# Channel mixing of a Fourier layer: three products per chunk against four products per pair of chunks

## The chip, the cores and the metric

The kernel runs as one program on one core of a Trainium2 chip. The metric is the device time of one execution in microseconds. TensorE (PE in the profile, PEld for its weight loads), VectorE (DVE), ScalarE (ACT), GpSimd (POOL) and SyncE (SP, which issues most transfers) each run their own instruction list in order and wait for each other through semaphores.

## The reference

Three layers follow one another. The change lies in the first, which works on eight batches of 3072 positions and 256 channels:

```python
X = np.fft.rfft(x, axis=1)                 # x: 8 x 3072 x 256
Yr = Xr @ w_r - Xi @ w_i + b_r             # w: 256 x 256
Yi = Xr @ w_i + Xi @ w_r + b_i
Yr = sign(Yr) * max(abs(Yr) - 0.01, 0)     # the same for Yi
y  = np.fft.irfft(Yr + 1j*Yi, n=3072, axis=1)
```

The second layer (`moe`) mixes all 24576 rows of y softly into 32 slots (softmax of `y @ phi` over the positions, and over the slots), sends the slots through eight small expert networks and spreads them back. The third (`moe2`) is a gated network with 1536 hidden units over all rows: RMS norm, `silu(g) * val`, `w_out`. The weights of `moe2` arrive as 64-bit floats.

## The kernel before

**Two stages.** `phase1` does everything up to the slots, without ever forming y: it computes the logits and the slot inputs from the spectrum. Short expert work follows (a class `Mid`, and the first part of `phase2`), and then `phase2` runs the gated network in 48 identical rounds. The change lies in `phase1` alone, apart from a buffer number in the middle part.

**What a batch goes through in `phase1`.** The transform is done in two steps. Step A (`emit_A`) multiplies 16 half tiles of x by a 96x96 table, as three products of split numbers: a value v is written as hi + lo, both in a rounded 32-bit format that TensorE takes fast (fp32r), and hi*hi, hi*lo, lo*hi are summed. `split_hi` rounds on ScalarE (line 218), `split_lo` subtracts on GpSimd (line 223). The result goes to DRAM and comes back turned (`load_B`). Step B (`emit_B`) multiplies it by the second table in full fp32, for six chunks q of 512 spectrum columns, each in two halves h of 128 channels. The mixing (`emit_M`) applies w_r and w_i, adds the bias and applies the threshold. `emit_T` turns the result for the slots, and `emit_L` makes the logits' spectrum with phi. A chain of some 30 small steps (`chain`) then turns logits into softmax weights and adds the batch to the running slot sums; it runs one batch behind, between the mixing of the next batch.

**The mixing in three products.** For each chunk, `emit_B` puts both the spectrum and the sum of its real and imaginary part through the split: line 281 writes lo, line 288 the sum `sm`, lines 291 and 294 the sum's hi and lo. Each of the 36 unit steps of a batch does six products of 256 columns (line 302): w_r on the sum into `psR`, and two difference matrices (`wh_d`, `wh_n`) into the two halves of `psI`, which has one buffer. ScalarE copies `psR` with the bias (lines 324, 325), VectorE adds `psI` (line 337), clips to +-0.01 (line 340), and GpSimd subtracts the clipped part (line 344), which is the threshold.

**What sets the order.** The code writes out each engine's order by hand. A loop of 288 unit steps u (36 per batch) issues a sixth of a chunk's mixing per step; `post` delays evacuations by one or more steps; the list at the end of `chain` puts each chain step at a step number. The chain's knot is: `dmax` (VectorE, line 429), `dpar` (GpSimd's maximum over partitions, line 433), `dmn` and `dsub` (VectorE, lines 442 to 452, which need it), `dexp` (ScalarE, line 457), `fa` (TensorE, line 509). The conversion of the 64-bit weights (`converter`, lines 132 to 153) is cut into 121 pieces. A running estimate of VectorE's load decides in which steps a piece is issued.

```python
return [(8, clear), ..., (16, L(dmax, 0, 32)), (17, L(dpar, 32)), (18, L(dmn, 32)),
        (18, L(dsub, 0, 32)), (19, L(dexp, 0, 32)), (19, alexp), (20, L(fa, 0, 16), 1), ...
```

Of the kernel before, what the change touches and what calls it, by code (L numbers as in the profile page):

```python
# [157 lines left out]
def phase1(tc, x, w_r, w_i, b_r, b_i, phi, t_d, t_bf, t_ci, t_ai, t_af, t_id,  # L158
# [46 lines left out]
    def split_hi(g, dve=False):  # L205
        b, i, h = g // 16, g // 2 % 8, g % 2
        if b == 0 and i % 2:

            if h == 0:
                xsp["t"] = xq_p.tile([128, 2, 2, 512], F32R, name="xq")[0:96]  # L210
            xs = xsp["t"][:, h, 0, :], xsp["t"][:, h, 1, :]
# [46 lines left out]
    def emit_B(b, q, h):  # L258

        t = bin_t[b, q]  # L260
        o = 2 if q else 0
        if h == 0:
            xq[b, q] = xq_p.tile([128, 2, 2, 512], F32R, name="xq")
            sq[b, q] = xq_p.tile([128, 2, 2, 258], F32R, name="sq")
        X, S = xq[b, q], sq[b, q]
# [5 lines left out]
        w4 = lambda a: a.rearrange("p (r j k) -> p r j k", j=4, k=32)  # L271
        hi, lo = [w4(X[:, k, h, :]) for k in range(2)]
        xi = xi_p.tile([128, 256], F32, name="xi")
        sm = xi_p.tile([128, 258], F32, name="sm")
# [22 lines left out]
        for k, f in enumerate((evac, rest, s_hi, s_lo)):  # L297
            post(f, 1 + k, int(k < 2))

    def products(ps, key, ch, V, w0, w1):  # L300
        for n, (w, k, h) in enumerate(((wh, 0, 0), (wh, 0, 1), (wl, 0, 0), (wl, 0, 1), (wh, 1, 0), (wh, 1, 1))):
            nc.tensor.matmul(out=ps, lhsT=w[key][:, h, 128 * ch:128 * ch + 128], rhs=V[:, k, h, w0:w1],  # L302
                             start=(n == 0), stop=(n == 5))

    def emit_M(b, q, m):

        X, S = xq[b, q], sq[b, q]
        ch, g = divmod(m, 3)
        if m == 0 and q % 2 == 0:
            if (b, q) == (NB - 1, 4):  # L310

                yy[b, 2] = mid.early.rearrange("p (a h f) -> p a h f", a=2, h=2), 0
            else:
                yy[b, q // 2] = y_p.tile([128, 2, 2, 514], F32, name="yy"), 2
        Y, y0 = yy[b, q // 2]
        o = 2 if q else 0
        Y = Y[:, q % 2, ch, o + y0 - 2:]
        if g == 0:
            ps = psR.tile([128, 512], F32, name="psR")
            products(ps[:, o:258], "r", ch, S, o, 258)  # L320
            v = mix["v"] = v_p.tile([128, 514], F32, name="v")

            def first():
                nc.scalar.activation(out=v[:, o:258], in_=ps[:, o:258], func=AF.Identity, bias=bias[:, 0, ch:ch + 1])
                nc.scalar.activation(out=v[:, 258:514], in_=ps[:, 2:258], func=AF.Identity, bias=bias[:, 1, ch:ch + 1])
            post(first)
            return
        if g == 1:
            mix["ps"] = psI.tile([128, 512], F32, name="psI")
            products(mix["ps"][:, 256:512], "d", ch, X, 0, 256)  # L330
            return
        ps, v = mix["ps"], mix["v"]
# [871 lines left out]
```

## Time and profile before

| what | value |
|---|---|
| three runs | 1872.07, 1874.18, 1877.80 us (median 1874.18) |
| the profiled execution | 1873.3 us, of which 1871.5 us are the span of the trace |
| busy in the span | PE 1744.1, weight loads 1548.1, DVE 1441.1, ACT 1154.0, POOL 408.2 us |
| start, up to the loop's first mixing product | 0 to 41.1 us |
| the loop of `phase1`, eight batches | 41.1 to 702.6 us: 66.4, 90.8, 85.9, 91.3, 89.6, 91.5, 85.7, 60.3 us |
| last chain, experts, start of the third layer | 702.6 to 786.1 us |
| the gated network | 786.1 to 1871.5 us, PE busy 1080.6 of 1085.4 us |

The boundaries of the batches are the start times of the first mixing product of each. The first batch has no chain beside it, the last no step A. The gated network has TensorE busy all the time at the full clock. In the loop no engine is busy all the time, and the granted clock of TensorE lies below 1.0.

### The profile page before, as it was taken

The numbers are of one execution on the slowest core, as the hardware profiler recorded it, in microseconds if no ns is written. First come the engines' busy times: TensorE is split into PE (matmuls) and PEld (weight loads), VectorE is DVE, ScalarE is ACT, GpSimd is POOL, SyncE is SP. The second block draws the span as 40 slices with busy tenths as digits, with TensorE's granted clock in tenths as the row PEclk, the third lists the DMA queues.
The fourth block names the chain that finished last, engine by engine and source line by source line (L and its number), as shares of the span: only waits on it lengthen the run. The fifth ranks groups of instructions, "written<-read, shape, count | busy, mean of one in ns | idle before, by whom it ended". The sixth has DMA issues, their size and how long they took to land.

```text
span 1871.5 us, 35164 instructions
## 1 busy us (share of the span) xinstructions
PE 1744.1 (93%) x13422; PEld 1548.1 (83%) x13422; DVE 1441.1 (77%) x2399; ACT 1154.0 (62%) x2451; POOL 408.2 (22%) x338
## 2 busy tenths in 40 slices
PE   7897889788888888999999999999999999999999
PEld 5776767576766764699999999999999999999998
DVE  5997988888897975677777777778777778778775
ACT  4764656464655543776676676666676676676653
POOL 3665555545564431100000000000000000000000
PEclk9998989898989999999999999999999999999999
DMA  9774635354554539702302302302302303202101
GB/s 238 225 190 119 178 111 164 113 164 124 156 161 136 164 104 308 215 24 62 61 24 63 60 23 63 60 24 63 63 25 67 64 23 75 48 24 57 28 19 35
DMA packets 134489, 183.57 MB, mean 98 GB/s; under 512 B 39232, under 2 KB 103248, under 8 KB 134320
## 3 DMA queue, kind: packets, MB, share of 16 engines
q1 hardware_dynamic: 133584, 179.36, 36.2%
q8 instruction: 105, 1.72, 0.4%
q0 software_dynamic: 624, 1.92, 0.4%
q14 instruction: 64, 0.52, 0.1%
q10 hardware_dynamic: 112, 0.04, 0.0%
HBM read 102.62 MB, written 66.06 MB: 90 GB/s over the span
## 4 chain that ended last, share of the span: by engine, by line
PE 58%; DVE 1%; DMA 1%; issue 0%; SPq 0%; ACT 0%; POOL 0%; DVEq 0%
PE pe L1101 21%; PE po L1101 21%; PE pg L1063 7%; PE pv L1065 7%; PE psx L848 1%; DMA wo<-wo_d 1%; DVE hl L97 1%; DMA cs<-ct_d 0%; PE pm L889 0%; PE pm L906 0%; PE psB L558 0%; PE psx L1101 0%; DVE h L1069 0%; SPq L855 0%; PE pm L848 0%
## 5 line engine op out<-in xcount | busy, mean ns | idle before, releaser
L1069 DVE TENSOR_TENSOR h<-s,pv 128x512 f32<-128x512 f32 x576 | 394.2, 685 | 268.4 <-ACT s L1067 267.6
L1067 ACT ACTIVATE s<-pg 128x512 f32<-128x512 f32 x576 | 344.5, 598 | 346.8 <-PE pg L1063 344.5
L1101 PE MATMUL pe<-wo,hh 128*128 128x256 f32 x2304 | 426.9, 279 | 0.3
L1101 PE MATMUL po<-wo,hh 128*128 128x256 f32 x2280 | 421.9, 279 | 0.0
L1101 PEld LDWEIGHTS pe<-wo,hh 128*128 128x128 f32 x2304 | 381.3, 188 | 42.2 <-DVE o L1117 3.0
L97 DVE TENSOR_TENSOR hl<-h,hh 128x512 fp32r<-128x512 f32 x572 | 405.9, 710 | 0.7 <-ACT s L1067 0.6
L96 ACT ACTIVATE hh<-h 128x512 fp32r<-128x512 f32 x576 | 359.4, 624 | 8.7 <-DVE h L1069 7.8
L1101 PEld LDWEIGHTS po<-wo,hh 128*128 128x128 f32 x2280 | 350.1, 188 | 4.4
L1101 PE MATMUL pe<-wo,hl 128*128 128x256 f32 x1152 | 321.0, 279 | 0.0
L1101 PE MATMUL po<-wo,hl 128*128 128x256 f32 x1140 | 317.7, 279 | 0.0
L1063 PE MATMUL pg<-cq,gst 128*128 128x512 f32 x576 | 229.8, 399 | 0.3 <-ACT s L1067 0.2
L1065 PE MATMUL pv<-cq,gst 128*128 128x512 f32 x576 | 228.0, 396 | 0.7 <-DVE h L1069 0.7
L1101 PEld LDWEIGHTS pe<-wo,hl 128*128 128x128 f32 x1152 | 216.1, 188 | 0.0
L1101 PEld LDWEIGHTS po<-wo,hl 128*128 128x128 f32 x1140 | 213.8, 188 | 0.0
L1039 POOL TENSOR_TENSOR c<-c,ss 128x768 f32<-128x768 f32 x7 | 10.9, 1553 | 842.1 <-DVE ss L1038 842.1
L223 POOL TENSOR_TENSOR xlo<-xraw,xhi 96x512 fp32r<-96x512 f32 x106 | 141.7, 1342 | 65.6 <-issue 28.6
L344 POOL TENSOR_TENSOR yy<-v,p 128x512 f32<-128x512 f32 (+1 forms) x92 | 123.4, 1341 | 114.7 <-DVE p L340 89.2
L302 PE MATMUL psI<-xq,wh_d 128*128 128x256 f32 x384 | 98.7, 340 | 51.9 <-DVE v L337 51.6
L302 PEld LDWEIGHTS psI<-xq,wh_d 128*128 128x128 f32 x384 | 64.7, 205 | 77.9 <-DVE v L337 61.1
L1065 PEld LDWEIGHTS pv<-cq,gst 128*128 128x128 f32 x576 | 108.5, 188 | 2.4 <-DVE h L1069 1.8
L245 ACT ACTIVATE asb<-psA 96x512 f32<-96x512 f32 x109 | 63.8, 586 | 73.9 <-PE psA L242 58.7
L1063 PEld LDWEIGHTS pg<-cq,gst 128*128 128x128 f32 x576 | 108.2, 188 | 1.3 <-ACT s L1067 1.1
(310 smaller groups left out, 2845.3 us busy)
## 6 DMA issues: line engine op xcount, KB each, us to landing
bin<-bounce SPq DMA_DIRECT2D x192, 128.0 KB, 4.0
bounce<-asb SPq DMA_DIRECT2D x59, 384.0 KB, 4.4
xraw<-in_x_dram SPq DMA_DIRECT2D x56, 384.0 KB, 3.9
ex<-in_moe_w_dram SPq DMA_DIRECT2D x16, 1024.0 KB, 10.6
out_dram<-o SPq DMA_DIRECT2D x124, 128.0 KB, 2.2
cs<-ct_d SPq DMA_DIRECT2D x32, 384.0 KB, 7.1
out_dram<-o SPq DMA_DIRECT2D x132, 64.0 KB, 1.7
ct_d<-ch SPq DMA_DIRECT2D x16, 384.0 KB, 3.3
```

The lines of the kernel that those rows point to most:

```text
L96: nc.scalar.activation(out=hi, in_=src, func=AF.Copy)
L97: (lo_eng or nc.vector).tensor_tensor(out=lo, in0=src, in1=hi.bitcast(F32), op=ALU.subtract)
L223: eng.tensor_tensor(out=lo, in0=v, in1=hi.bitcast(F32), op=ALU.subtract)
L245: nc.scalar.activation(out=asb[b, i][:, 512 * h:512 * h + 512], in_=ps, func=AF.Copy)
L302: nc.tensor.matmul(out=ps, lhsT=w[key][:, h, 128 * ch:128 * ch + 128], rhs=V[:, k, h, w0:w1], start=(n == 0), stop=(n == 5))
L344: eng.tensor_tensor(out=Y, in0=v[:, o:514], in1=p[:, o:514], op=ALU.subtract)
L848: nc.tensor.matmul(out=ps[:, 256 * k:256 * k + 256], lhsT=v[:, 128 * (n + k):128 * (n + k) + 128], rhs=sst, start=True, stop=True)
L1063: nc.tensor.matmul(out=pg, lhsT=gst[:, 128 * fb:128 * fb + 128], rhs=v, start=True, stop=True)
L1065: nc.tensor.matmul(out=pv, lhsT=gst[:, 1536 + 128 * fb:1536 + 128 * fb + 128], rhs=v, start=True, stop=True)
L1067: nc.scalar.activation(out=s, in_=pg, func=AF.Silu)
L1069: nc.vector.tensor_tensor(out=h, in0=s, in1=pv, op=ALU.mult)
L1101: nc.tensor.matmul(out=ps, lhsT=a[:, ts], rhs=w[:, fb, :], start=(fb == 0 and k == 0), stop=(fb == 11 and k == 2))
```

## The change

- **Mixing.** Four products instead of three, on pairs of chunks: real and imaginary part, each from w_r and from w_i (or its negative `wh_n`), in groups of 12 products of 512 columns. The groups go through two buffers `psM`, which replace `psR` and `psI`. A unit step now issues four products of 512 columns instead of six of 256. The sums `sm`, their split and the tiles for them are gone.
- **Threshold.** ScalarE writes relu(ps + b - 0.01) straight from PSUM (`first`), and VectorE writes min(ps + b + 0.01, that) from PSUM over it (`end`). Clip and GpSimd's subtraction are gone. The columns of frequency 0 and 1536, which the three-product form treated inside the sums, get four tiny fp32 products of their own (`emit_0`).
- **Conversion.** Its last one or two operations go from GpSimd to VectorE. The rule for when to issue a piece has other numbers: 21 pieces a batch in batches 1 to 5 (16 before, 22 in batch 5), 15 in batch 0 (11 before), and the last of the 121 is issued at step 216 (249 before).
- **Chain.** The steps stand at other numbers: `dmax` 12, `dpar` 13, `dmn` and `dsub` 18, `dexp` 19, `fa` 22 and 23. `dsub` now writes its result turned, so that `fa` reads 512 neighbouring elements instead of elements 32 apart.
- **Loop.** Steps A, B, T and L stand at other places within 12 steps instead of 6. One of the sixteen expert tiles (1 MB each) is loaded after the loop instead of near its end.

```diff
@@ converter
-            nc.gpsimd.tensor_tensor(out=w, in0=w, in1=p.bitcast(F32), op=ALU.mult)
+            v.tensor_tensor(out=w, in0=w, in1=p.bitcast(F32), op=ALU.mult)
...
-                nc.gpsimd.tensor_tensor(out=w, in0=w, in1=h, op=ALU.subtract)
+                v.tensor_tensor(out=w, in0=w, in1=h, op=ALU.subtract)
@@ emit_B
         def evac():
             nc.scalar.activation(out=hi, in_=v, func=AF.Copy)
-            nc.scalar.activation(out=w4(xi), in_=v[:, 2:4], func=AF.Copy)
 
         def rest():
             nc.vector.tensor_tensor(out=lo, in0=v, in1=hi.bitcast(F32), op=ALU.subtract)
...
-            nc.vector.tensor_tensor(out=w4(sm[:, 2:258]), in0=v[:, 0:2], in1=w4(xi), op=ALU.add)
-
-        def s_hi():
-            nc.scalar.activation(out=S[:, 0, h, o:258], in_=sm[:, o:258], func=AF.Copy)
-
-        def s_lo():
-            nc.vector.tensor_tensor(out=S[:, 1, h, o:258], in0=sm[:, o:258], in1=S[:, 0, h, o:258].bitcast(F32), op=ALU.subtract)
@@ emit_M
+        ways = (("r", ri), ("i" if ri else "n", 1 - ri))
+        cs = slice(128 * ch, 128 * ch + 128)
+        if m % 3 < 2:
+            h = m % 3
+            terms = [(w[key][:, h, cs], X[:, 0, h, part]) for key, part in ways for w in (wh, wl)]
+        else:
+            terms = [(wh[key][:, h, cs], X[:, 1, h, part]) for h in range(2) for key, part in ways]
+        for n, (w, v) in enumerate(terms):
+            nc.tensor.matmul(out=ps, lhsT=w, rhs=v, start=(m % 3 == 0 and n == 0), stop=(m % 3 == 2 and n == 3))
...
-        def add():
-            nc.vector.tensor_tensor(out=v[:, 2:514], in0=ps, in1=v[:, 2:514], op=ALU.add)
-
-        def clip():
-            nc.vector.tensor_scalar(out=p[:, o:514], in0=v[:, o:514], scalar1=LAM, scalar2=-LAM, op0=ALU.min, op1=ALU.max)
+        def first():
+            nc.scalar.activation(out=Y, in_=ps[:, o:512], func=AF.Relu, bias=b_lo[:, ri, ch:ch + 1])
 
         def end():
-            eng = nc.vector if (b, q) == (NB - 1, 5) else nc.gpsimd
-            eng.tensor_tensor(out=Y, in0=v[:, o:514], in1=p[:, o:514], op=ALU.subtract)
+            nc.vector.scalar_tensor_tensor(out=Y, in0=ps[:, o:512], scalar=b_hi[:, ri, ch:ch + 1], in1=Y, op0=ALU.add, op1=ALU.min)
@@ chain
-            v = S["d"].rearrange("p (n s) -> p n s", s=32)[:, :, s0:s1]
+            v = S["d"].rearrange("p (s n) -> p n s", n=32)[:, :, s0:s1]
...
-                nc.tensor.matmul(out=ps, lhsT=af, rhs=v[:, k:k + 16], start=True, stop=True)
+                nc.tensor.matmul(out=ps, lhsT=af, rhs=S["d"][:, 32 * k:32 * k + 512], start=True, stop=True)
...
-                    (16, L(dmax, 0, 32)), (17, L(dpar, 32)), (18, L(dmn, 32)), (18, L(dsub, 0, 32)), (19, L(dexp, 0, 32)),
+                    (12, L(dmax, 0, 32)), (13, L(dpar, 32)), (14, cmax), (15, csub), (18, L(dmn, 32)), (18, L(dsub, 0, 32)),
@@ loop
-        load = max(0.0, load + fixed[(u + 1) % 6] + chained.get((u + 1) % 36, 0.0) - (1.7 if u < 6 * (T - 17) else 1.82))
+        load = max(0.0, load + fixed[(u + 1) % 12] + chained.get((u + 1) % 36, 0.0) - pace)
```

**The order on GpSimd around the maximum.** The kernel before, in a middle batch (ISA rows belong to the maximum over partitions, `mb<-mx`; `xlo` is `split_lo`, `yy` the end of the threshold, `cvw` the conversion, `ch<-ch,mc` a later chain step):

```order
L223 TENSOR_TENSOR xlo<-xraw,xhi 96x512
L344 TENSOR_TENSOR yy<-v,p 128x512
L433 ISA
L433 ISA mb<-mx 128x32
L223 ISA
L223 TENSOR_TENSOR xlo<-xraw,xhi 96x512
L344 TENSOR_TENSOR yy<-v,p 128x512
L223 TENSOR_TENSOR xlo<-xraw,xhi 96x512 x2
L344 TENSOR_TENSOR yy<-v,p 128x512
L144 TENSOR_TENSOR cvw<-cvw,cva 128x256
```

The changed kernel at the same place:

```order
L226 TENSOR_TENSOR xlo<-xraw,xhi 96x512 x11
L429 ISA
L429 ISA mb<-mx 128x32
L226 ISA
L226 TENSOR_TENSOR xlo<-xraw,xhi 96x512
L465 TENSOR_TENSOR ch<-ch,mc 96x1024
L226 TENSOR_TENSOR xlo<-xraw,xhi 96x512 x3
L479 TENSOR_TENSOR ch<-ch,sc 96x1024
L226 TENSOR_TENSOR xlo<-xraw,xhi 96x512
L489 TENSOR_TENSOR ch<-ch 96x1024
```

The end of the threshold and the conversion have left GpSimd. Beside the maximum and three chain steps only `split_lo` is left on it.

**The order on VectorE around the wait for that maximum.** The kernel before, from `dmax` to `dsub` (`mn<-mb` is the first instruction that needs the maximum, `v` and `p` belong to the mixing, `cva` to the conversion):

```order
L429 TENSOR_REDUCE mx<-ch 96x32
L132 TENSOR_SCALAR cva<-cvraw 128x256
L133 TENSOR_SCALAR cva<-cva 128x256
L134 TENSOR_SCALAR cva<-cva 128x256
L337 TENSOR_TENSOR v<-psI,v 128x512
L340 TENSOR_SCALAR p<-v 128x512
L442 TENSOR_TENSOR mn<-mb,mn 128x32
L444 TENSOR_TENSOR al<-mn 128x32
L452 TENSOR_TENSOR ch<-ch,mn 96x1024
L281 TENSOR_TENSOR xq<-psB,xq 128x512
```

The changed kernel, the last rows up to the same instruction:

```order
L132 TENSOR_SCALAR cva<-cvraw 128x256
L133 TENSOR_SCALAR cva<-cva 128x256
L134 TENSOR_SCALAR cva<-cva 128x256
L323 SCALAR_TENSOR_TENSOR yy<-psM,b_hi,yy 128x512
L376 STREAM_TRANSPOSE lf<-psT 128x256
L136 SCALAR_TENSOR_TENSOR cva<-cvraw,cva 128x256
L138 TENSOR_SCALAR cve<-cvraw 128x256
L139 TENSOR_SCALAR cve<-cve 128x256
L280 TENSOR_TENSOR xq<-psB,xq 128x4x128
L438 TENSOR_TENSOR mn<-mb,mn 128x32
L440 TENSOR_TENSOR al<-mn 128x32
L448 TENSOR_TENSOR ch<-ch,mn 96x32x32
```

In the changed kernel `dmax` (line 425 there) stands 18 instructions ahead of `mn<-mb`, five unit steps after it; in the kernel before it stands six instructions ahead, two unit steps.

## Rows read from the trace of the kernel before

**Rows 1.** Busy time by stretch: batch 0, 4, 7, the part after the loop.
```profile
core 0: us, PE busy (x) PEld busy (x) DVE busy (x) ACT busy (x) POOL busy (x), PEclk, DMA share, GB/s
41.10:107.50 66.40, 58.90 (x442) 50.86 (x442) 59.35 (x100) 47.98 (x110) 41.67 (x38) 1.00 0.83 225
...
375.50:465.10 89.60, 74.80 (x611) 60.12 (x610) 75.75 (x130) 50.80 (x110) 47.95 (x39) 0.90 0.50 140
...
642.30:702.60 60.30, 52.90 (x530) 43.49 (x529) 42.71 (x76) 27.41 (x63) 21.35 (x17) 0.97 0.48 148
702.60:786.10 83.50, 70.88 (x555) 40.94 (x553) 51.57 (x89) 41.73 (x89) 14.50 (x11) 0.98 0.99 292
```

**Rows 2.** The same view of batch 4 by chunk: the third, fourth and fifth.
```profile
400.00:411.30 11.30, 10.68 (x74) 8.86 (x72) 11.02 (x17) 9.04 (x20) 6.05 (x5) 1.00 0.57 145
411.30:434.20 22.90, 17.20 (x117) 11.90 (x115) 14.42 (x25) 9.60 (x22) 6.98 (x7) 0.78 0.22 73
434.20:450.50 16.30, 12.08 (x94) 10.85 (x91) 15.36 (x28) 7.66 (x17) 10.06 (x9) 0.79 0.57 160
```

**Rows 3.** Waits from 100 to 580 us: total us, times, longest.
```profile
PE psI L302 <- DVE v L337: 42.1, 26, 4.2
...
PE psC L509 <- ACT ch L457: 17.3, 5, 5.2
...
DVE mn L442 <- POOL mb L433: 16.7, 4, 6.5
```

**Rows 4.** Timeline of batch 4: start, us, instruction, idle before it and its releaser.
```profile
417.15 0.45 POOL L433 PARTITION_ALL_REDUCE mb<-mx  x1 [6.38 <-PE psI L302]
417.63 0.19 DVE L442 TENSOR_TENSOR mn<-mb,mn 128x32 f32<-128x32 f32 x1 [4.10 <-POOL mb L433]
...
419.22 1.06 ACT L457 ACTIVATE ch<-ch 96x1024 f32<-96x1024 f32 x1 [5.16 <-DVE ch L452]
...
420.33 2.08 PE L509 MATMUL psC<-ch,af 96*128 96x512 f32 x2 [3.70 <-ACT ch L457]
...
424.74 1.25 POOL L223 TENSOR_TENSOR xlo<-xraw,xhi 96x512 fp32r<-96x512 f32 x1 [7.14 <-issue]
```

**Rows 5.** Timeline of batch 4, TensorE at the full clock: transposes, step B, logits, chain.
```profile
410.04 0.60 PE L365 MATMUL psT<-ident,yy 128*128 128x128 f32 x4
...
410.48 1.06 PE L268 MATMUL psB<-bf,bin 128*128 128x128 f32 x8
...
411.29 0.49 PE L302 MATMUL psR<-sq,wh_r 128*128 128x256 f32 x2
...
414.66 1.07 PE L377 MATMUL psT<-yy,ph 128*32 128x256 f32 x16
...
415.66 0.50 PE L302 MATMUL psI<-xq,wh_n 128*128 128x256 f32 x2
...
435.98 0.86 PE L531 MATMUL psC<-bf,ch 128*32 128x128 f32 x24
```

**Rows 6.** Chain that ended last, start of the gated network: start, us, what.
```profile
786.66 0.70 PE pe L1101 x6
...
788.07 0.23 PE pg L1063
```

**Rows 7.** Groups by line up to 760 us: count, busy, mean ns, idle before.
```profile
L337 DVE TENSOR_TENSOR v<-psI,v 128x512 f32<-128x512 f32 x96 | 65.3, 680 | 3.2 <-PE psI L302 2.9 <-PE psB L268 0.2
...
L340 DVE TENSOR_SCALAR p<-v 128x512 f32<-128x512 f32 x80 | 52.5, 656 | 37.4 <-POOL yy L344 29.3 <-DVE v L337 0.5
...
L294 DVE TENSOR_TENSOR sq<-sm,sq 128x256 fp32r<-128x256 f32 x80 | 49.9, 624 | 3.4 <-ACT sq L291 3.4
...
L288 DVE TENSOR_TENSOR sm<-psB,xi 128x256 f32<-128x256 f32 x96 | 39.8, 415 | 0.4
...
L133 DVE TENSOR_SCALAR cva<-cva 128x256 int32<-128x256 int32 x36 | 36.4, 1011 | 1.2
...
L143 DVE SCALAR_TENSOR_TENSOR cvw<-cvr,cve 128x256 f32<-128x256 int32 x36 | 21.3, 591 | 1.2
```

More of the change, by code (lines that the diff above doesn't have):

```diff
@@ L165, in phase1 @@
     dpool = P(st_c, "bounce", 2, DRAM)
-    psA, psB, psR, psI, psT, psC = (P(st_c, n, b, PSUM) for n, b in
-                                    (("psA", 1), ("psB", 2), ("psR", 1), ("psI", 1), ("psT", 1), ("psC", 1)))
+    psA, psB, psM, psT, psC = (P(st_c, n, b, PSUM) for n, b in
+                               (("psA", 1), ("psB", 2), ("psM", 2), ("psT", 1), ("psC", 1)))
     ch_p, yt_p, sm_p = P(st_c, "ch", 5), P(st_c, "yt", 10), P(st_c, "sm", 2)
@@ L209, in split_hi @@
             if h == 0:
[L210 to L211 removed]
+                xsp["t"] = xq_p.tile([128, 2, 2, 2, 512], F32R, name="xq")[0:96]
+            xs = xsp["t"][:, h, 0, 0, :], xsp["t"][:, h, 1, 0, :]
         else:
@@ L260, in emit_B @@
         t = bin_t[b, q]
[L261 to L265, printed above, removed]
+        if h == 0 and q % 2 == 0:
+            xq[b, q // 2] = xq_p.tile([128, 2, 2, 2, 512], F32R, name="xq")
+        if h == 0 and q == 0:
+            x0[b] = x0_p.tile([128, 2, 2], F32, name="x0")
         ps = psB.tile([128, 512], F32, name="psB")
@@ L270, in emit_B @@
         v = ps.rearrange("p (j r k) -> p r j k", r=4, k=32)
[L271 to L274, printed above, removed]
+        hi, lo = [xq[b, q // 2][:, k, h].rearrange("p a f -> p (a f)").rearrange("p (r z j k) -> p r z j k", r=4, z=2, k=32)[:, :, q % 2]
+                  for k in range(2)]
         def evac():
             nc.scalar.activation(out=hi, in_=v, func=AF.Copy)
-            nc.scalar.activation(out=w4(xi), in_=v[:, 2:4], func=AF.Copy)
         def rest():
@@ L295, in emit_B @@
         if h == 1:
             bin_t.pop((b, q))
[L297 to L312, printed above, removed]
-            else:
[L314 to L326, printed above, removed]
-            return
[L328 to L332, printed above, removed]
-        products(ps[:, 0:256], "n", ch, X, 256, 512)
-        p = p_p.tile([128, 514], F32, name="p")
-        def add():
-            nc.vector.tensor_tensor(out=v[:, 2:514], in0=ps, in1=v[:, 2:514], op=ALU.add)
-        def clip():
-            nc.vector.tensor_scalar(out=p[:, o:514], in0=v[:, o:514], scalar1=LAM, scalar2=-LAM, op0=ALU.min, op1=ALU.max)
-        def end():
-            eng = nc.vector if (b, q) == (NB - 1, 5) else nc.gpsimd
-            eng.tensor_tensor(out=Y, in0=v[:, o:514], in1=p[:, o:514], op=ALU.subtract)
-            if q == 0:
-                nc.gpsimd.tensor_copy(out=Y[:, 258:259], in_=Y[:, 0:1])
-            if ch == 1:
-                xq.pop((b, q))
-                sq.pop((b, q))
-        for k, f in enumerate((add, clip, end)):
-            post(f, (1, 1, 2)[k], (0, 0, 1)[k])
@@ new lines, in emit_0, with first, end @@
+    def emit_0(b):
+        X = x0.pop(b)
+        ps = psB.tile([128, 512], F32, name="psB")
+        for ch in range(2):
+            for h in range(2):
+                nc.tensor.matmul(out=ps[:, 2 * ch:2 * ch + 2], lhsT=wf[:, h, 128 * ch:128 * ch + 128], rhs=X[:, h, :],
+                                 start=(h == 0), stop=(h == 1))
+        Y = yy[b, 0]
+        def first():
+            for ch in range(2):
+                nc.scalar.activation(out=Y[:, :, ch, 0], in_=ps[:, 2 * ch:2 * ch + 2], func=AF.Relu, bias=b_lo[:, 0, ch:ch + 1])
+        def end():
+            for ch in range(2):
+                nc.vector.scalar_tensor_tensor(out=Y[:, :, ch, 0], in0=ps[:, 2 * ch:2 * ch + 2], scalar=b_hi[:, 0, ch:ch + 1],
+                                               in1=Y[:, :, ch, 0], op0=ALU.add, op1=ALU.min)
+        post(first, 1)
+        post(end, 2)
@@ L353, in ysl @@
     def ysl(Y, qs, h, ri, par):
-        f = Y[1] + 256 * ri + 128 * par
-        return Y[0][:, qs, h, f:f + 128]
+        return Y[:, ri, h, 256 * par + 128 * qs.start:256 * par + 128 * qs.stop]
     def emit_T(b, q, ri, ps=None):
@@ L569, in busy @@
         def busy(n):
-            ps = bank(psI, "psI")
+            ps = bank(psM, "psM")
             for _ in range(n):
@@ L635, in load_bf @@
         eng.dma_start(out=bf[:, 4 * q:4 * q + 4], in_=t_bf[:, 4 * q:4 * q + 4])
-    banks = [(psA, "psA"), (psI, "psI"), (psB, "psB"), (psT, "psT"), (psB, "psB"), (psR, "psR")]
+    banks = [(psA, "psA"), (psM, "psM"), (psB, "psB"), (psT, "psT"), (psB, "psB"), (psM, "psM")]
     def split_x(g):
@@ L662, in phase1 @@
     load_B(0, 2)
-    for c in range(-5, 0):
+    for c in range(-6, 0):
         clock[0] = c
```

154 lines of the change are left out of this document (91 added, 63 removed).

## The prediction

> **What bounds the kernel now.** I read the busy time by stretch first. The gated network after 786.1 us is untouched and full of TensorE work, so the change can act in the loop (41.1 to 702.6 us) and in the part after it [rows 1]. In batch 4, which stands for the middle ones, 89.6 us pass with VectorE busy 75.75, TensorE 74.80, ScalarE 50.80 and GpSimd 47.95, and the granted clock is 0.90 on the mean, a mix of the levels 2.4 and 1.2 GHz [rows 1]. No engine is full, so waits decide. By chunk, the fourth takes 22.9 us where the third takes 11.3, with the clock at 0.78 [rows 2].
>
> The waits name two places. TensorE waits for VectorE to free `psI`, 42.1 us from 100 to 580 us, that is in 5.4 batches, 7.8 us a batch [rows 3]. And once a batch the chain closes in on itself: GpSimd stands still for 6.38 us before the maximum over partitions and 7.14 us after it, VectorE waits 4.10 us for it, ScalarE behind that 5.16 us, TensorE behind that 3.70 us [rows 4], and after it the clock is low for a while [rows 2]. In all five batches in this stretch TensorE waits at that place, 17.3 us together [rows 3].
>
> **What TensorE needs in a batch.** At the full clock six products of 256 columns take 0.70 us and one of 512 takes 0.23 [rows 6]; four transposes take 0.44 (410.04 to 410.48), eight instructions of step B 0.81, one `emit_L` 1.0, 24 instructions of `fb` 0.86 [rows 5]; two of the four `fa` instructions take 2.08 [rows 4]. A batch before:
> mixing 216 x 0.117 = 25.3; A 48 x 0.23 = 11.0; B 96 x 0.10 = 9.7; T 12 x 0.44 = 5.3; L 3 x 1.0 = 3.0; `fa` 4.2; the rest of the chain, priced by form, `fb` and the equally large `binv` 1.7 each, the slot products 3.0 at the price of L, `ainv` 0.9, so 7.3. Sum 65.8 us. So 23.8 of the 89.6 us are waits and half clock.
>
> **The change part by part.**
>
> *Four products.* 144 x 0.23 = 33.1 us replace 25.3: +7.8 a batch, on TensorE, which no other work hides once it is the bound.
>
> *`fa` from neighbouring elements.* 4.2 us become 4 x 0.23 = 0.9, if 512 columns then cost what they cost elsewhere: -3.3. Ends: 0 (the price stays) and -3.3. I take the low price, since the other products with neighbouring elements all have it. `emit_0` adds eight tiny instructions, between 0.1 and 0.9 us (at most the transposes' 0.11 each), I take 0.6. TensorE's need: 65.8 + 7.8 - 3.3 + 0.6 = 70.9 us.
>
> *VectorE.* Twelve each of lines 288, 294, 337 and 340 go: 12 x (0.415 + 0.624 + 0.680 + 0.656) = 28.5 us [rows 7]. Twelve `end` come, like line 337 a read of PSUM and one of SBUF over 512 elements: 8.2. Conversion: seven products of 0.59 (line 143, same size) that GpSimd did, 4.1, and five more pieces of three instructions at 0.59, 8.9. The turned `dsub` and the small ones, 1.5. So 75.75 - 28.5 + 8.2 + 4.1 + 8.9 + 1.5 = 70.0. From it comes off what VectorE is held by GpSimd: line 133 takes 1.01 us for 256 elements, line 288 0.415 for as many, and 0.6 of that I read as time held. GpSimd's share falls from 0.54 to some 0.35 (48 us less 21 for 12 subtractions and the conversion, over about 77), so a third of 7 x 5 x 0.6 goes: -7. VectorE 63, between 60 and 70: below TensorE's 70.9, but close.
>
> The Trainium skill ("SBUF — State Buffer", section "SBUF: two separate sides") says that VectorE and GpSimd share one port pair as an exclusive lock, and that a VectorE instruction with two inputs from SBUF takes part in it too. That speaks against moving the conversion's products to VectorE; line 143 with its two such inputs takes 0.59 us against line 288's 0.415, a smaller penalty than line 133's, so the trace agrees in kind. By the rule at its worst each of the seven would wait for a whole `xlo` (1.25 us), 9 us a batch instead of 1.
>
> *ScalarE and GpSimd.* ScalarE loses more than it gains and has 39 us free in batch 4. On GpSimd only `split_lo` and the chain are left; each is wanted two A steps later, which is 36/16 x 2 = 4.5 unit steps, about 9 us at 77 us a batch.
>
> *The chain's new places.* `dpar` is issued five unit steps before `dmn` instead of one, some 10 us against 2.5 (89.6 over 36). GpSimd's 6.38 us before the result lie inside that, and the 7.14 us after it inside the 9 us of the `split_lo` on either side. So VectorE's 4.10 us, and behind it ScalarE's and TensorE's, go. The chunk's excess over the third is 11.6 us, of which 4.0 is `fa`'s own price, so 7.6 us a batch. The price if the cover is gone is rival C. The first load of a batch has five unit steps from the last evacuation of A as before, but shorter ones; I count a microsecond for it among the waits that stay.
>
> *`psM` with two buffers.* `end` is issued two unit steps before its buffer is needed again, so VectorE may lag by some 4 us. That takes the 7.8 us at `psI`. What is late next is VectorE during conversion, and step T at the one-buffer `psT`.
>
> *After the loop.* One more tile of 1 MB goes into a stretch whose transfers are busy at 0.99 and run at 292 GB/s [rows 1]: 3.6 us, between 0 (hidden behind the experts' products) and 3.6; I take 3.6. The start: the first mixing product needs two chunks of step B, +1 us.
>
> **The sum.** Of the 23.8 us of waits and half clock 7.6 and 7.8 go; of the 8.4 left I keep 6, since two engines near each other still trip over the conversion's lumps. A batch with chain and conversion: 70.9 + 6 = 77 us.
> Batches 1 to 5: 449.1 become 385. Batch 6, now without conversion: 85.7 become 74. Batch 0, without chain and with few waits to lose: 66.4 + 7.8 - 4 = 70. Batch 7: 60.3 + 7.8 - 3.3 and its stop at the maximum less, 60. The loop: 661.5 become 589, -72.5. With +4.6 outside: 1873.3 - 67.9 = 1805 us, against the profiled execution's own 1873.3. That lies 0.9 below the median of the runs, which changes nothing here.
>
> **Rivals.**
>
> A, *TensorE alone is the bound*: waits of 1 to 2 us a batch. For it: two buffers everywhere on the mixing, and the clock stays high if TensorE never pauses (third chunk: busy 10.68 of 11.3 us, clock 1.00) [rows 2]. Against: `psA` and `psT` keep one buffer. 5 x 72 + 71 + 67 + 58 = 556 for the loop: 1773 us.
>
> B, *VectorE becomes the bound while it converts*: 70 us of work in order with waits at today's ratio (75.75 of 89.6) is 83 to 84 us a batch. For it: three conversion instructions in a row, over 1 us each when GpSimd is active, and the pieces are now denser. Against: that ratio contains the two waits that go. 5 x 84 + 76 + 72 + 61 = 629: 1845 us.
>
> C, *slower: GpSimd's stop hits TensorE directly*. GpSimd is away for 6.38 + 7.14 us around each maximum, and that stays. If it gets to it late, the `split_lo` behind it come late, TensorE stands at step A, and the half clock follows as in the fourth chunk. 13.5 us exposed, some 5 us for the low clock after it, the 6 that stay: 70.9 + 24.5 = 95 us a batch. It decides the sign from 18.7 us of waits a batch. 5 x 95 + 90 + 74 + 66 = 705: +48, 1921 us. Against: only `split_lo` depends on GpSimd now, and it is two steps ahead. The Trainium skill ("GPSIMD Engine Reference", section "2.1 Instruction dispatch") says that the first call of freshly loaded GpSimd code pays about 6 us with nothing in the profile; the trace agrees, with 6.38 and 7.14 us and no instruction in them, and the change removes neither.
>
> D, *nothing moves*: what the waits give back, the fourth product takes (+7.8), and the order stumbles elsewhere by as much: within 0.3%.
>
> **Chances.** Forecast 0.55, A 0.16, B 0.21, C 0.05, D 0.03. The forecast's own range is 1785 to 1825; the range for all takes in most of A and B: 1768 to 1850. A measurement of this kernel tells about 0.3% from no change. Faster 0.92, same 0.03, slower 0.05.
>
> **What would show it.** Right: batches of 75 to 80 us from one first mixing product to the next; TensorE busy over 0.93 of them at a clock of 0.97 or more; `fa` at a quarter of its time; no wait of VectorE for `mb`; GpSimd's two idle stretches still there, each of 6 to 7 us, with no TensorE wait for `xlo` behind them. Wrong: batches over 82 us with TensorE waiting for `end` or for lo of step B (B), waits for `xlo` over 5 us a batch (C), or a product of 512 columns at more than 0.24 us.

## The result and the profile after

The changed kernel takes 1804.03 us, the median of four runs (1802.13 to 1805.98), against 1875.99 us before (1872.07 to 1882.23): ratio 0.9614, 95% interval 0.9583 to 0.9644. The forecast was 1805. The profiled execution took 1805.45 us, 1803.7 of them in the trace.

Busy time by stretch, the changed kernel: batches 0, 3, 4 and 7, the part after the loop, the gated network (columns as in [rows 1]).

```profile
44.40:112.10 67.70, 66.26 (x378) 52.66 (x377) 39.88 (x78) 40.82 (x76) 27.20 (x26) 1.00 0.84 240
...
266.30:344.20 77.90, 76.02 (x545) 57.10 (x544) 64.51 (x111) 43.10 (x78) 28.25 (x20) 1.00 0.60 171
344.20:421.30 77.10, 75.82 (x545) 57.10 (x544) 63.53 (x103) 43.98 (x82) 27.81 (x20) 1.00 0.62 176
...
569.70:629.90 60.20, 58.33 (x465) 43.44 (x464) 28.68 (x43) 19.69 (x33) 6.69 (x4) 1.00 0.41 127
629.90:718.00 88.10, 73.49 (x565) 45.26 (x564) 51.22 (x87) 43.09 (x94) 14.51 (x11) 0.91 0.99 290
718.00:1803.70 1085.70, 1080.93 (x8134) 1026.82 (x8133) 802.71 (x1298) 714.02 (x1492) 26.62 (x14) 1.00 0.20 45
```

The batches last 67.7, 76.4, 77.8, 77.9, 77.1, 77.0, 71.4 and 60.2 us: the loop went from 661.5 to 585.5 us, -76.0. Around it the start grew by 3.3 us and the part after the loop by 4.6; the gated network stayed (1085.4 and 1085.7). The sum, -67.8, is the difference of the two spans. In the middle batches TensorE is now busy 75.8 to 76.0 of 77 to 78 us at a clock of 1.00. Before, it was busy 74.80 of 89.60 at 0.90 [rows 1], partly with instructions that ran at half the clock. By the granted clock, 105.8 us of the loop lay at 1.2 GHz before, none now; such time is called half clock below.

All waits of TensorE in the changed kernel from 112 to 498 us, the five middle batches (total us, times, longest):

```profile
PE psM L313 <- DVE xq L280: 2.2, 2, 1.1
PE psC L526 <- DVE ch L510: 1.1, 2, 0.5
PE psA L245 <- ACT asb L248: 0.9, 5, 0.2
PE psT L361 <- DVE lf L376: 0.9, 1, 0.9
PE psM L313 <- DVE yy L323: 0.6, 2, 0.4
PE psA L245 <- POOL xlo L226: 0.5, 1, 0.5
PE psB L270 <- DMA bin<-bounce: 0.4, 1, 0.4
```

That is 6.6 us in five batches, some 1.3 a batch. Of the 42.1 us at `psI` [rows 3] 0.6 are left at `psM` (`yy`), of the 17.3 us behind the maximum nothing.

The changed kernel around the maximum in batch 3 (timeline, as in [rows 4]):

```profile
292.66 2.04 DVE L425 TENSOR_REDUCE mx<-ch 96x32 f32<-96x1024 f32 x1
...
295.56 0.45 POOL L429 PARTITION_ALL_REDUCE mb<-mx  x1 [6.31 <-DVE yy L323]
...
298.05 0.42 DVE L144 TENSOR_TENSOR cvw<-cvw,cva 128x256 f32<-128x256 f32 x1
...
301.83 0.18 DVE L438 TENSOR_TENSOR mn<-mb,mn 128x32 f32<-128x32 f32 x1
...
302.15 2.00 DVE L448 TENSOR_TENSOR ch<-ch,mn 96x1024 f32<-96x1024 f32 x1
...
302.82 1.06 PE L270 MATMUL psB<-bf,bin 128*128 128x128 f32 x8
...
303.63 0.48 PE L313 MATMUL psM<-xq,wh_r 128*128 128x512 f32 x1
303.68 1.50 POOL L226 TENSOR_TENSOR xlo<-xraw,xhi 96x512 fp32r<-96x512 f32 x1 [7.67 <-ACT yy L320]
...
303.94 0.40 PE L313 MATMUL psM<-xq,wl_r 128*128 128x512 f32 x1
```

GpSimd still stops, 6.31 us before the maximum and 7.67 after it, but the result is there at 296.0 and is wanted at 301.83, so VectorE no longer waits, and TensorE hardly waits for the `xlo` behind it (0.5 us once in five batches).

TensorE in the same batch around two `fa` (line 504):

```profile
312.43 1.02 PE L504 MATMUL psC<-ch,af 96*128 96x512 f32 x2
312.88 0.79 PE L313 MATMUL psM<-xq,wh_r 128*128 128x512 f32 x1
313.52 0.40 PE L313 MATMUL psM<-xq,wh_i 128*128 128x512 f32 x1
313.75 0.39 PE L313 MATMUL psM<-xq,wh_r 128*128 128x512 f32 x1
313.99 0.39 PE L313 MATMUL psM<-xq,wh_i 128*128 128x512 f32 x1
```

Starts tell the price better than the busy times, since matmuls overlap, but only among their like. There a product of 512 columns starts 0.23 us before the next, the instructions of step B follow each other at 0.112 us, and the two `fa` at 0.43 (the pair's 1.02 less the 0.592 of one, below). At the border of two kinds the starts mislead: the first product behind `fa` seems to take 0.64, the first behind step B (303.63 above) 0.31. But from the first `fa` (312.43) to the second product (313.52) pass 1.09 us, which is 2 x 0.43 + 0.23, and from step B's first instruction (302.82) to the second product (303.94) 1.12 us, which is 8 x 0.112 + 0.23 to within 0.01. So the product costs there what it costs among its like; its start is recorded early, and the time that seems to be its own belongs to the instructions ahead of it.

Groups by line up to 760 us, the changed kernel (as in [rows 7]):

```profile
L144 DVE TENSOR_TENSOR cvw<-cvw,cva 128x256 f32<-128x256 f32 x36 | 29.9, 830 | 1.2
L143 DVE SCALAR_TENSOR_TENSOR cvw<-cvr,cve 128x256 f32<-128x256 int32 x36 | 26.1, 726 | 1.2
L133 DVE TENSOR_SCALAR cva<-cva 128x256 int32<-128x256 int32 x36 | 17.7, 492 | 1.2
L504 PE MATMUL psC<-ch,af 96*128 96x512 f32 x28 | 14.3, 592 | 0.0
...
L323 DVE SCALAR_TENSOR_TENSOR yy<-psM,b_hi,yy 128x512 f32<-128x512 f32 x60 | 43.4, 723 | 14.4 <-ACT yy L320 14.4
```

Line 133 fell from 1.01 [rows 7] to 0.49 us, with GpSimd busy 28 of 77 us instead of 48 of 90. The product that came to VectorE (line 144) takes 0.83 on the mean, but no single one does: of the 36, the 21 with no GpSimd operation beside them take 0.42 to 0.43, as in the row at 298.05, and the 15 with one beside them 1.39 to 1.41. Not every line gained: line 143 rose from 0.59 to 0.73. The Trainium skill ("SBUF — State Buffer", section "SBUF: two separate sides") has a VectorE instruction with two inputs from SBUF and GpSimd exclude each other at a shared port; the two durations of line 144 agree in kind.

### The profile page after: what moved, and what is told of

The parts are those of the page before. It is cut to its first block, busy times and chain, and to the rows that moved or that the text cites. A ratio compares the mean times of both kernels' runs of the same rounds, so it can differ in the third digit from the quotient of the medians.

```text
span 1803.7 us, 33098 instructions
## 1 busy us (share of the span) xinstructions
PE 1761.6 (98%) x12910; PEld 1530.9 (85%) x12910; DVE 1294.7 (72%) x2125; ACT 1087.1 (60%) x2178; POOL 246.9 (14%) x182
## 4 chain that ended last, share of the span: by engine, by line
PE 67%; DVE 2%; DMA 2%; issue 1%; SPq 0%; ACT 0%; POOL 0%; DVEq 0%; ACTq 0%
PE pe L1105 22%; PE po L1105 22%; PE pg L1067 7%; PE pv L1069 7%; PE psM L313 3%; PE psx L852 1%; PE psB L270 1%; DMA bin<-bounce 1%; DMA wo<-wo_d 1%; DMA cs<-ct_d 1%; DVE hl L97 1%; PE pm L893 0%; PE psA L245 0%; PE pm L910 0%; PE psT L373 0%
## 5 line engine op out<-in xcount | busy, mean ns | idle before, releaser
L313 PE MATMUL psM<-xq,wh_r 128*128 128x512 f32 x384 | 173.4, 452 | 3.3 <-DVE xq L280 2.2
L277 ACT ACTIVATE xq<-psB 128x512 fp32r<-128x512 f32 x96 | 57.2, 596 | 118.0 <-PE psB L270 118.0
L280 DVE TENSOR_TENSOR xq<-psB,xq 128x512 fp32r<-128x512 f32 x96 | 65.8, 686 | 77.2 <-ACT xq L277 77.0
L270 PE MATMUL psB<-bf,bin 128*128 128x128 f32 x768 | 105.4, 281 | 8.5 <-DMA bin<-bounce 7.8
L270 PEld LDWEIGHTS psB<-bf,bin 128*128 128x128 f32 x768 | 95.2, 194 | 19.7 <-issue 15.8
```

Of the source, the lines that this page charges most:

```text
L270: nc.tensor.matmul(out=ps[:, 128 * j:128 * j + 128], lhsT=t[:, j, 128 * h:128 * h + 128], rhs=bf[:, 4 * q + j, :], start=True, stop=True)
L313: nc.tensor.matmul(out=ps, lhsT=w, rhs=v, start=(m % 3 == 0 and n == 0), stop=(m % 3 == 2 and n == 3))
```

## The experiments

Each kernel is the changed one with one edit, unless it says before; the intervals are of the ratio to the kernel before. Differences in us are between medians; the kernel before itself had medians from 1874.07 to 1875.99 us in these comparisons, so one or two microseconds say nothing.

**Was it the maximum's stop that cost time in the kernel before? The kernel before, without the maximum over partitions.**

```diff
-            nc.gpsimd.partition_all_reduce(out_ap=S["mb"][:, 0:w], in_ap=mx[:, 0:w], channels=128, reduce_op=ReduceOp.max)
+            nc.vector.tensor_copy(out=S["mb"][:, 0:w], in_=mx[:, 0:w])
```

> The kernel before with the maximum over partitions left out (each partition keeps its own maximum, a tiny copy on VectorE), so that GpSimd never stops for it. Theory 1: what cost the kernel before its time at this place is GpSimd's stop of 13.5 us, with the end of the threshold and split_lo queued behind it, wherever in the chain it is issued: 7 to 11 us (wait and half clock) in each of seven batches, -45 to -80 us. Theory 2: VectorE's load of 75 us a batch sets the length, the stop only shifts waits: 0 to -15 us.

Measured 1826.29 us, 0.9734 (0.9719 to 0.9748): -49.7, or 7.1 us for each of the seven chains that have a batch beside them, as theory 1 had it, at its lower end. The half clock in the loop fell from 105.8 to 47.8 us. TensorE's other wait, from 100 to 580 us, stayed:

```profile
PE psI L302 <- DVE v L337: 45.7, 30, 3.1
```

**The same edit in the changed kernel.**

> The changed kernel with the same part left out. Theory 1: with the threshold off GpSimd and split_lo two steps ahead, the stop is fully covered: 0 to -8 us. Theory 2: the stop still costs there, through split_lo or through VectorE's wait for the maximum: -20 us or more.

1804.13 us, 0.9621 (0.9607 to 0.9635): no gain, theory 1. In batches 1 to 5, 77.5 us on the mean against 77.2, the stop costs nothing (TensorE waits 8.8 us there, against 6.6). The equal totals say less than that, for two differences cancel in them: the loop is 6.6 us longer here (3.4 of them in batch 0, which has no maximum), and the part after it 6.3 us shorter. There the changed kernel has no cover for the last chain's maximum, as its waits of TensorE from 630 to 760 us and its chain that ended last show:

```profile
PE psM L526 <- DVE z_run L540: 4.7, 1, 4.7
```

```profile
647.33 3.15 issue
650.48 1.91 POOL ch L465
```

GpSimd stands still for 10.18 us behind that maximum, and TensorE's 4.7 us stand behind it; without the maximum this wait is gone. How much of the 6.3 us it made is not shown.

**Do the chain's places alone hide it? The kernel before, with the maximum two steps earlier.**

```diff
-                    (16, L(dmax, 0, 32)), (17, L(dpar, 32)), (18, L(dmn, 32)), ...
+                    (14, L(dmax, 0, 32)), (15, L(dpar, 32)), (18, L(dmn, 32)), ...
```

> The kernel before with one edit: the maximum over partitions and the step ahead of it are issued two unit steps earlier (14 and 15 instead of 16 and 17), what needs it stays at 18. Theory 1: the closed knot (VectorE waits 4.1 us for GpSimd, ScalarE and TensorE behind it, half clock after it) costs 7.6 us in each of the seven batches with a chain: -35 to -55 us, about 1830 us. Theory 2: VectorE's total work bounds the kernel before, and the stop only moves its waiting elsewhere: 0 to -12 us.

1904.33 us, 1.0157 (1.0141 to 1.0172): slower by 29.5 us than the kernel before in the same comparison, against both theories. VectorE no longer waits for `mb`, but from 100 to 580 us it and others wait for what GpSimd does behind the stop:

```profile
DVE p L340 <- POOL yy L344: 56.6, 5, 13.0
...
ACT v L324 <- POOL yy L344: 44.6, 5, 10.3
...
PE psA L242 <- POOL xlo L223: 30.3, 5, 7.4
```

Once per chain the end of the threshold (`yy`) is late by the whole stop, 13.0 us at most. VectorE's clip waits for it, since `p` has one buffer, ScalarE's copy waits for one of the two buffers of `v`, and `xlo` comes late for TensorE.

**The changed kernel with the maximum at its old places.**

```diff
-                    (12, L(dmax, 0, 32)), (13, L(dpar, 32)), (14, cmax), (15, csub), (18, L(dmn, 32)), ...
+                    (14, cmax), (15, csub), (16, L(dmax, 0, 32)), (17, L(dpar, 32)), (18, L(dmn, 32)), ...
```

> The changed kernel with the knot closed again: the maximum at 16 and 17 instead of 12 and 13, what needs it at 18. Theory 1: the knot costs as much here as in the kernel before, 4 to 8 us in each of seven batches: +28 to +55 us. Theory 2: with two psM buffers and 13 us of VectorE's time free in a batch, most of a 4 us wait of VectorE is absorbed: 0 to +12 us.

1829.5 us, 0.976 (0.9741 to 0.9779): +25.5, 3.6 us a chain, between the theories. Batches 1 to 5 take 78.8 to 83.1 us, and ScalarE waits once per chain for VectorE's subtraction (112 to 498 us):

```profile
ACT ch L453 <- DVE ch L448: 18.7, 5, 4.8
```

So the places are needed too, but at the old ones the changed kernel loses half of what the kernel before lost (25.5 against 49.7 us).

**The conversion's last products back on GpSimd.**

```diff
-            v.tensor_tensor(out=w, in0=w, in1=p.bitcast(F32), op=ALU.mult)
+            nc.gpsimd.tensor_tensor(out=w, in0=w, in1=p.bitcast(F32), op=ALU.mult)
...
-                v.tensor_tensor(out=w, in0=w, in1=h, op=ALU.subtract)
+                nc.gpsimd.tensor_tensor(out=w, in0=w, in1=h, op=ALU.subtract)
```

> The changed kernel with the conversion's last one or two operations back on GpSimd. Theory 1: VectorE (64 us of 77) is so close behind TensorE that 4 us less on it take away half of the 1 to 2 us of TensorE's waits a batch, and GpSimd is idle: -8 to +3 us. Theory 2: GpSimd's operations hold VectorE's single-source instructions (each 0.77 us, 7 a batch), and transfers of the results wait for GpSimd: +8 us or more.

1851.45 us, 0.9868 (0.9853 to 0.9882): +47, inside theory 2's "+8 us or more", but by another path than it gave. The batches with conversion and chain take 84 to 88 us. Waits from 112 to 498 us:

```profile
DVE cva L132 <- POOL cvw L144: 39.6, 13, 8.8
...
PE psT L361 <- DVE lf L376: 30.6, 6, 9.9
```

The product stands in GpSimd's queue behind the stop: in batch 1 the maximum starts at 143.4 us, the next `xlo` at 152.3 and the product at 153.5. VectorE's next conversion piece waits for its buffer (8.8 us, ending at 154.3), `lf` queues behind that on VectorE, and step T on TensorE waits for it at the single `psT`: 9.9, 9.2 and 8.7 us in batches 1 to 3. Batches 4 and 5, which wait elsewhere, are the shorter ones (84 us).

**One buffer for the mixing's result instead of two.**

```diff
-                               (("psA", 1), ("psB", 2), ("psM", 2), ("psT", 1), ("psC", 1)))
+                               (("psA", 1), ("psB", 2), ("psM", 1), ("psT", 1), ("psC", 1)))
```

> The changed kernel with one psM buffer. Every group of products then has to wait until ScalarE (0.69 us) and VectorE (0.73 us) have read the group before. Theory 1: this wait, at least 12 x 1.4 = 17 us a batch and more where VectorE lags, is what the second buffer saves: +120 us or more, slower than the kernel before. Theory 2: it costs what one psI buffer cost the kernel before, 7.8 us a batch: +55 to +75 us.

1998.03 us, 1.0659 (1.064 to 1.0678): +194, slower than the kernel before by 122, as theory 1 had it. TensorE's wait from 112 to 498 us:

```profile
PE psM L313 <- DVE yy L323: 72.4, 38, 5.9
```

That stretch has 3.8 batches here, so 19 us a batch. Besides, 99 us of the loop ran at half the clock.

**The end of the threshold done twice on VectorE (the values stay the same).**

```diff
-            nc.vector.scalar_tensor_tensor(out=Y, in0=ps[:, o:512], ...)
+            for _ in range(2):
+                nc.vector.scalar_tensor_tensor(out=Y, in0=ps[:, o:512], ...)
```

> The changed kernel with every end of the threshold done twice (the second changes nothing in the values): 12 x 0.73 = 8.8 us more VectorE work a batch, 64.5 becomes 73 of 77 us. Theory 1 (TensorE bounds, VectorE has real slack): 0 to +12 us in all. Theory 2 (VectorE's work with waits at a busy share of 0.85 bounds, so that 73 us need 86): +45 us or more.

1828.04 us, 0.975 (0.9736 to 0.9765): +24, between the theories. Twelve more instructions at 0.723 us are 8.7 us a batch; batches 1 to 3 grew to 82.2 to 84.2 us, batch 4 by 1.4, batches 5 and 6 did not grow. TensorE's waits from 112 to 498 us:

```profile
PE psM L313 <- DVE xq L280: 7.5, 3, 3.1
PE psM L313 <- DVE yy L324: 7.1, 7, 1.4
```

With 73 us of work VectorE makes batches 1 to 3 longer. Since 8.7 us more work cost 4 to 6 us there, I estimate that at its own 64 us it lies some 3 us a batch short of doing so.

**48 of the 144 products a batch left out.**

```diff
-            terms = [(w[key][:, h, cs], X[:, 0, h, part]) for key, part in ways for w in (wh, wl)]
+            terms = [(w[key][:, h, cs], X[:, 0, h, part]) for key, part in ways for w in (wh,)]
```

> The changed kernel without the products of the spectrum's hi with the weights' lo: 8 of each chunk pair's 24 per group are left out, 48 products of 512 columns a batch, 48 x 0.234 = 11.2 us of TensorE work (its output misses that correction). Theory 1 (TensorE is the bound, VectorE stands right behind it at 64 us of work, which with its waits passes as some 73 to 75 us): batches 1 to 5 fall only to 72 to 75 us, batches 0, 6 and 7 by 6 to 11 us each; 1755 to 1775 us. Theory 2 (TensorE alone is the bound, VectorE has real slack): every batch falls by 10 to 11 us; 1715 to 1727 us.

1763.5 us, 0.9414 (0.9397 to 0.9431): -40.5, in theory 1's range, but not for its reason. Batches 1 to 5 take 70.4 to 73.2 us (-5.8 on the mean, for 11.2 us of work less). The window of its batch 3, and its largest wait of TensorE from 112 to 498 us:

```profile
251.10:321.90 70.80, 66.28 (x497) 49.47 (x496) 63.01 (x111) 42.83 (x78) 27.70 (x20) 0.98 0.66 188
```

```profile
PE psA L245 <- POOL xlo L226: 12.6, 5, 2.9
```

Of the half of the gain that is missing the largest part went not to VectorE (2.2 us of waits for `lf`, 2.0 for `xq`) but to GpSimd's stop, which with shorter batches reaches TensorE through `xlo`: 12.6 of 24.8 us of waits. Another part went to 34 us of half clock in the loop.

**`fa` and its input in the old layout.**

```diff
-            v = S["d"].rearrange("p (s n) -> p n s", n=32)[:, :, s0:s1]
+            v = S["d"].rearrange("p (n s) -> p n s", s=32)[:, :, s0:s1]
...
-                nc.tensor.matmul(out=ps, lhsT=af, rhs=S["d"][:, 32 * k:32 * k + 512], start=True, stop=True)
+                nc.tensor.matmul(out=ps, lhsT=af, rhs=v[:, k:k + 16], start=True, stop=True)
```

> The changed kernel with fa again reading elements 32 apart (and dsub writing in its old order). Theory 1: TensorE alone bounds the batches of the changed kernel, so every microsecond of its own work shows in full: fa took about 1.0 us per instruction before and takes about 0.4 in the changed kernel, 4 instructions and 7 chains inside the loop, so 2.4 us a batch, +14 to +20 us, about 1820 us. Theory 2: waits for VectorE set the length of a batch, TensorE's own work has slack: +0 to +5 us (VectorE even saves 0.8 us a batch on dsub).

1809.76 us, 0.9655 (0.9639 to 0.9671): +5.7, close to theory 2; the intervals of this ratio and of the changed kernel's overlap. `fa` (line 505 here) and the subtraction by line, and then batch 2 by stretch:

```profile
L505 PE MATMUL psC<-ch,af 96*128 96x512 f32 x28 | 26.3, 1030 | 0.0
...
L448 DVE TENSOR_TENSOR ch<-ch,mn 96x1024 f32<-96x1024 f32 x6 | 7.3, 1214 | 0.0
```

```profile
188.50:265.80 77.30, 77.12 (x545) 57.36 (x544) 63.98 (x113) 42.62 (x77) 28.26 (x20) 1.00 0.62 174
```

A pair of `fa` takes 0.87 us more here from start to start, 1.75 a batch. TensorE is busy 77.12 of 77.30 us and waits 0.2 us a batch. Batches 1 to 5 are as long as in the changed kernel, where waits of 1.3 us a batch stand in place of the longer `fa`. That the turned subtraction (2.00 us against 1.21) makes those waits is not shown; with the turn on ScalarE, below, they stay. What the new layout gains lies in the last two batches (73.1 and 62.9 us here, 71.4 and 60.2 there), most surely in batch 6, which has no conversion and takes 71.4 us in six other variants of the changed kernel too: there the price of 1.75 us shows almost in full.

**The turn on ScalarE instead of VectorE.**

```diff
+            S["x"] = ch_p.tile([128, 1024], F32, name="ch")[0:96]
...
-            nc.scalar.activation(out=v, in_=v, func=AF.Exp)
+            nc.scalar.activation(out=S["d"].rearrange("p (s n) -> p s n", n=32)[:, s0:s1],
+                                 in_=S["x"].rearrange("p (n s) -> p s n", s=32)[:, s0:s1], func=AF.Exp)
```

(The slot products of the expectation are `fa`.)

> The changed kernel with the turn of the logits' layout moved from the subtraction on VectorE (2.00 us turned, 1.21 us straight in the kernel before) to the exponential on ScalarE, through one more tile; the slot products still read neighbouring elements. Theory 1 (the turned subtraction delays the evacuation of step B behind it, and TensorE waits there for the 0.5 to 1 us a batch that is seen): batches 1 to 5 become 76 to 76.5 us, 1796 to 1800 us in all. Theory 2 (that wait is passed on to the next place, or the turned exponential on ScalarE costs as much): 1802 to 1806 us.

1807.57 us (1802.73 to 1813.8), 0.9648 (0.9623 to 0.9673): no gain, theory 2. TensorE's waits from 112 to 498 us are 7.4 us, against 6.6 in the changed kernel. The exponential takes 2.13 us instead of 1.05, and in the last chain the extra tile has to wait for a buffer that a GpSimd step behind the maximum's stop sets free:

```profile
L453 ACT ACTIVATE ch<-ch 96x1024 f32<-96x1024 f32 x7 | 14.9, 2129 | 0.0
...
L505 PE MATMUL psB<-ch,af 96*128 96x512 f32 x2 | 2.1, 1142 | 12.3 <-ACT ch L453 12.3
```

```profile
657.05 1.07 ACT L453 ACTIVATE ch<-ch 96x512 f32<-96x512 f32 x1 [12.75 <-POOL ch L466]
```

**The rows of the gated network's batch 1 prepared later.** In the changed kernel, after the loop, TensorE's timeline has:

```profile
715.44 0.76 PE L852 MATMUL psx<-sst,cs 128*128 128x256 f32 x2 [4.33 <-DMA cs<-ct_d]
716.00 0.63 PE L1105 MATMUL pe<-wo,hh 128*128 128x256 f32 x2
...
720.02 0.39 PE L1105 MATMUL pe<-wo,hh 128*128 128x256 f32 x2
```

A wait of 4.33 us for a load (the expectation below put it at 6), and the same two products at 0.63 us instead of 0.39 for a while: the granted clock is 1.2 GHz from 713.1 to 720.0 us, so it fell during the wait. The edit leaves the loads where they were and issues the products that need them later.

```diff
-                if b + 1 < NB and 1 <= r <= 3 and fb % 3 == 1:
+                late = 12 * (r - 1) + fb - 5
+                if b == 0 and late % 2 == 0 and 0 <= late < 24:
+                    prep_x(1, late)
+                elif 0 < b < NB - 1 and 1 <= r <= 3 and fb % 3 == 1:
```

> The changed kernel with the preparation of the gated network's batch 1 rows issued later inside the rounds of batch 0. In the part after the loop of the changed kernel TensorE waits 6 us for a load there and then runs at half the clock for 6.8 us. Theory 1 (that load is only asked for too early; the transfers catch up later without hurting): the wait and its low clock go, -6 to -9 us, 1795 to 1798 us. Theory 2 (the transfers, busy at 0.99, set this stretch, and the wait only moves): 1802 to 1806 us.

1799.22 us (1798.44 to 1801.72), 0.9604 (0.959 to 0.9618): 4.8 us below the changed kernel's median, close to theory 1. The part after the loop, to the same length of the gated network:

```profile
629.00:711.50 82.50, 70.23 (x563) 42.71 (x562) 50.33 (x86) 42.20 (x90) 14.51 (x11) 0.96 1.02 306
```

82.5 us instead of 88.1, and the wait for `cs` is gone. The ranges of the runs don't overlap, the intervals of the two ratios do, so the gain is shown by the stretch rather than by the total.

**Three edits together**: this one, the turn on ScalarE, and step A's 16th half tile through its usual buffer.

```diff
-            emit_A(16, bank(*banks[16 % 6])[0:96])
+            emit_A(16)
```

> The changed kernel with three edits together: the turn of the layout on ScalarE, the later preparation of batch 1's rows, and the loop's first product of a batch 16th half tile through the usual buffers of step A. Theory 1 (the three gains are at different places and add up): -10 to -18 us against the changed kernel, 1786 to 1794 us. Theory 2 (neither wait is real, both move on): 1800 to 1806 us.

1805.66 us, 0.9634 (0.9616 to 0.9652): no better than the changed kernel. The turn's wait in the last chain is back (11.9 us), and the gain of the later preparation is lost with it. The best version found is the one with the later preparation alone.

## Why the prediction was right, and which of its steps were not

The time was met within 1 us. Of the steps behind it some held, and two large ones were off by nearly as much in opposite directions. The loop gained 3.5 us more than forecast (-76.0 against -72.5), the rest lost 3.3 more (+7.9 against +4.6).

**TensorE's need, 70.9 us: too small.** Measured 75.9 of busy time. The mixing is not the reason: 144 products at 0.234 us, their distance among their like, are 33.7 us against 33.1. The prediction named "a product of 512 columns at more than 0.24 us" as a sign against it; the mean from start to start is 0.263, but that takes in the borders between kinds and the waits. Too small were the fp32 instructions: step B at 96 x 0.112 = 10.8 against 9.7, since the 0.81 for eight [rows 5] was read up to the early start of the product behind them; `fa` and the equally large `ainv` at 4 x 0.43 = 1.7 each against 0.9; `emit_L` at 3.4 against 3.0. With 0.6 of the mixing, 0.3 of step A and 0.2 of `emit_0`, less 0.3 where the price was too high, that is 3.9 of the 5.0 us; the rest has no place that the trace shows.

**Waits, 6 us: too many.** 1.3 were left. So the middle batch came out as 75.9 + 1.3 instead of 70.9 + 6. The two errors are in part one: step B, `ainv` and `emit_L` were priced as low in the batch before (65.8), and what that sum lacked went into its 23.8 us of waits and half clock, of which the 6 were kept. That the rest cancels so well is luck. What bounds the changed loop is rival A's case, TensorE alone, at a price per batch that A did not have. The kernels with `fa`'s old layout (77.30 us, busy 77.12) and without the maximum (no gain in batches 1 to 5) say the same. Not much lies behind it: 11.2 us of TensorE's work less shortened the batches by 5.8.

**The maximum, 7.6 us a batch: right in size, incomplete in cause.** 7.1 measured. "The chain's new places" do not free it alone: an earlier maximum makes the kernel before slower by 29.5 us, because the threshold's end then stands in the stop. In the changed kernel (`dmax` stands six unit steps ahead of `dmn` there, `dpar` five) the places are worth 25.5 us; for the rest GpSimd had to be emptied as well.

**The conversion's products on VectorE: booked as a cost of 4.1 us a batch, in truth worth 47 us in all.** The prediction counted their work and not the buffer for which VectorE would have waited behind GpSimd's stop. Its main rule for GpSimd, that "only `split_lo` and the chain are left", holds because of this part.

**`psM` with two buffers**: right, and with one the change would have been slower than before. That a second `psI` alone would have freed the 7.8 us in the kernel before is not shown.

**`fa`, -3.3 us: too much.** 0.592 us busy instead of about 1.03, 1.75 a batch from start to start, and in batches 1 to 5 waits take its place. "`fa` at a quarter of its time" did not come. The 0.23 was the price of products in the rounded format, and `fa` is in full fp32; step B's rows [rows 5] had a price for that, 0.81 for eight times 128 columns, so 0.41 for 512, close to the 0.43 measured.

**VectorE, 63 us:** 59.8 to 64.9 measured in batches 1 to 5, and close behind TensorE as said: 8.7 us more work lengthened batches 1 to 3 by 4 to 6 us.

**Outside the loop:** +4.6 after it against 3.6 forecast. Whether the tile's transfer makes it is not shown. TensorE waits 4.3 us for `cs` there, 2.6 in the kernel before, and 15.1 us of the stretch are half clock, 3.4 before. With the tile still loaded there and one preparation later, the stretch takes 82.5 us, less than the 83.5 before, so the tile need not cost anything. The start grew by 3.3, not 1; its cause is open.

**Rivals.** B fell: all waits of TensorE for VectorE are 4.8 us in five batches. C fell for this kernel, but it is near: the kernel with 48 products less runs into it (`xlo`, 12.6 us), and an earlier maximum in the kernel before turned the sign, in part by it (`xlo`, 30.3 us). D fell: the time moved by 72 us.

## What to carry to other kernels

When an engine stops once per round for a fixed time, moving its result earlier is not enough: list what else stands in its queue behind the stop, and how many buffers each of its readers has. Work moved to a busier engine can pay for itself many times if it leaves such a queue.

Price a matmul from start to start within a run of its own kind and number format. At the border of two kinds a start is recorded early, and a run that is priced up to there comes out short: eight instructions of step B at 0.81 us instead of 0.90. And a remainder of "waits" holds whatever the priced work lacks. Once TensorE was busy 98% of a batch, a shorter instruction on VectorE gained nothing there (the turn on ScalarE).
